# A shorter run-up on TensorE and a shorter way to the score bias, in a planned attention-plus-MLP kernel

## The chip, the cores and the metric

The kernel runs on one core of one Trainium2 chip. The metric is the device time of one execution in microseconds (us). TensorE (PE) multiplies; its weight loads are listed apart as PEld. VectorE is DVE, ScalarE is ACT, GpSimd is POOL, and SyncE (SP) issues nearly all DMAs.

## The reference

Windowed attention over 8 batches of 8 heads, 576 tokens of 64 numbers, is followed by a two-layer MLP with a squared ReLU over all 4608 tokens. Condensed:

```python
scores = scale * np.matmul(q, k.transpose(0, 1, 3, 2))
mask = np.abs(pos[:, None] - pos[None, :]) <= 32
scores = np.where(mask, scores, -1000000000.0)
attn = softmax(scores)                       # rows
x = (attn @ v) as [4608, 512]
h = x @ w_in                                 # 512 -> 2048
g = s * np.maximum(h, 0) ** 2 + b
out = g @ w_out                              # 2048 -> 512
```

## The kernel before

Nothing in this kernel is a loop on the chip. Python code calls `add(...)` once for each piece of work (a "task"), with the engine that does it, an estimated cost in ns, the tiles it reads and writes, and a key that breaks ties. `_Graph.plan` then plays the tasks through on a clock of estimates: it always takes the task that can start earliest, and of several the one with the lowest key. The order in which the plan takes them becomes the fixed program order of each engine, and `_Graph.emit` puts a semaphore wait where a task needs the result of another engine. So a changed cost or dependency moves tasks in the queues, and an engine that waits holds everything behind it in its own queue. Two rules of `emit` matter here: PE does not wait for PE, since it works in order; and each POOL task waits for the POOL task before it.

The start of the program is the part that the change touches.

- **Run-up.** DVE writes the all-ones tile ONESW (L463), and PE multiplies it with itself 26 times, 128 columns each (L486), into bank 1 of W. Nobody reads the result.
- **Constant tiles.** The helper `band` (L468 to L475) makes a 0/1 band by two POOL affine selects from ONESW. It makes the identity IDENT (for transposes) and MASK (the window of 32 on either side). From MASK, POOL computes NEG (L484), which is 0 inside the window and -1e38 outside. Copies of MASK with cuts (L501, L504) are for later units. Ahead of all this POOL fills two scratch tiles of `early` (L1028, L1029).
- **Batch 0, pairs of heads.** For each of four pairs, q and k are loaded (L579), cast to bf16 (`turn_pair`, L588 and L589: q on ACT once, then on POOL; k on DVE), transposed on PE against IDENT into W bank 0 for q and bank 1 for k (L595), and copied out as QT by ACT (L600) and KT by DVE (L601).
- **Scores of batch 0** (`pair_scores`). PE first writes NEG into the score bank: IDENT times NEG, two matmuls of 512 columns (L817), into SC for pairs 0 and 2 and into O for pairs 1 and 3; two more open AVN for the odd last tile (L822). The scores are then added on top (L826), so that the exponential (`first_exp`, L848) needs no mask. Batch 1 and later multiply the exponential by MASK on DVE (L853, L716).
- **Units of batch 0** (`first_units`). Five units of attention times V (L742), with a reciprocal and a scaling on DVE (L764, L766), a transpose on PE (L773) and a copy to XT on ACT (L781). V is loaded by L562 and cast by L571.
- **First MLP blocks.** Four short token blocks (96, 128, 128, 160 tokens) run the first layer (`s1`, L973, then L980 on ACT and L982 on DVE) while the weights still arrive: w_in and w_out in eight loads each (L534), cast on POOL (L537). `early` runs their second layer (L1022), and L1030, a sum over all of w_out for the constant term of the output, needs all eight w_out casts.
- **Batch 1 and later.** The pairs of batch 1 come through the same staging buffers (eight of them) as the weights, so an SP load waits until the cast of the earlier user is done. From batch 2 on, loads are paced by finished units, and PE alternates between L973 and L991, the second layer.

Of the kernel before, what the change touches and what calls it, by code (L numbers as in the profile page):

```python
# [9 lines left out]
ALU = mybir.AluOpType  # L10
# [6 lines left out]
WIN = 32  # L17
NPAIR = H // 2
NTILE = S // 64
# [31 lines left out]
TURN_DVE = ()  # L51
WARM = 26
LEAST = 2.0 ** -60
# [263 lines left out]
def bass_sliding_window_symmetric__then__act_starrelu_kernel(  # L317
# [23 lines left out]
    with ExitStack() as es:  # L341
# [125 lines left out]

        def band(tile, src, res, lo, hi, key, step=1):  # L468
            add("pool",
                lambda e: e.affine_select(tile, src, pattern=[[1, 128]],  # L470
                                          compare_op=ALU.is_ge, fill=0.0, base=-lo,
                                          channel_multiplier=-step),
                300, reads=["ONESW"], writes=[res], key=key)
            add("pool",
                lambda e: e.affine_select(tile, tile, pattern=[[-1, 128]],  # L475
                                          compare_op=ALU.is_ge, fill=0.0, base=hi,
                                          channel_multiplier=step),
                300, reads=[res], writes=[res], key=key)

        band(IDENT[:, :], ONESW[:, :], "IDENT", 0, 0, -98)  # L480
        for p0 in (0, 64):
            band(MASK[p0:p0 + 64, :], ONESW[p0:p0 + 64, :], ("MASK", 0, p0), 0, 64, -96)

        add("pool", lambda e: e.tensor_scalar(NEG[:, :], MASK[:, :], 1.0, FAR, ALU.subtract, ALU.mult), 250,  # L484
            reads=[("MASK", 0, 0), ("MASK", 0, 64)], writes=["NEG"], key=-95.5)
        add("pe", [lambda e: e.matmul(W[:, 1, 0:128], lhsT=ONESW[:, :], rhs=ONESW[:, :], start=True, stop=True)] * WARM,  # L486
            110.0 * WARM, reads=["ONESW"], writes=[("W", 1)], key=-99)

# [10 lines left out]

        for i, cuts in ((1, ((0, 96), (64, 0))), (2, ((64, 96),)), (3, ((0, 0),))):  # L500
            add("pool", lambda e, i=i: e.tensor_copy(MASKS[i][:, :], MASK[:, :]), 250,  # L501
                reads=[("MASK", 0, 0), ("MASK", 0, 64)], writes=[("MASK", i, 0), ("MASK", i, 64)], key=0.0)
            for p0, c0 in cuts:
                add("pool", lambda e, i=i, p0=p0, c0=c0: e.memset(MASKS[i][p0:p0 + 64, c0:c0 + WIN], 0.0), 150,  # L504
                    writes=[("MASK", i, p0)], key=0.0)
        for i in range(2):
# [77 lines left out]
        def turn_pair(b, name, pr, key, banks, eng, slack):  # L584
# [11 lines left out]
                view[p0:p0 + 64, i, :], nat[p0:p0 + 64, i * 64:i * 64 + 64], IDENT[p0:p0 + 64, p0:p0 + 64])  # L596
                for i in range(ROWS) for p0 in (0, 64)], 500.0, reads=[("NAT", ni), "IDENT"], writes=[res], key=key)
            flat = QT[slot][:, pr, WIN:WIN + S] if name == "q" else KT[slot][:, pr, :]
# [209 lines left out]
        def pair_scores(b, pr):  # L808
# [5 lines left out]
            if b == 0:  # L814
                wide = NEG.rearrange("p (one c) -> p one c", one=1)
                four = wide.to_broadcast((128, 4, 128))
                add("pe", [lambda e, hp=hp: e.matmul(bank[:, hp, :].rearrange("p (a c) -> p a c", a=4), lhsT=IDENT[:, :],  # L817
                                                     rhs=four, start=True, stop=True, skip_group_check=True)
                           for hp in (0, 1)], 440, reads=["NEG", "IDENT"], writes=[(name, 0), (name, 1)], key=-80.0 + pr)
                if pr == 0:  # L820
                    half = wide[0:64].to_broadcast((64, 4, 128))
                    add("pe", [lambda e, hp=hp: e.matmul(  # L822
                        AVN[0:64, hp, :].rearrange("p (a c) -> p a c", a=4), lhsT=IDENT[0:64, 0:64],
                        rhs=half, start=True, stop=True, skip_group_check=True) for hp in (0, 1)],
                        440, reads=["NEG", "IDENT"], writes=[("AVN", 0), ("AVN", 1)], key=-79.5)
            fns = [lambda e, j=j, hp=hp: e.matmul(  # L826
# [6 lines left out]
            key = (-30.0 if b == 0 else due(1, 0) - 3.5) + (1.0 if b == 0 else 0.1) * pr  # L833
            add("pe", fns, 450.0 if b == 0 else 500.0, reads=[("QT", b, x, pr) for x in range(NTILE)] +
                [("KT", b, x, pr) for x in range(NTILE)] + [("QTZ", b, 0), ("QTZ", b, WIN + S)],
# [49 lines left out]
        def attention():  # L885
# [15 lines left out]
            for t in ORDER0:  # L901
# [3 lines left out]
                else:  # L905
                    w("in", t - 8)
            first_units()
            for i, src in enumerate((moe_s, moe_b)):
                add("sp", lambda e, i=i, src=src: e.dma_start(SROW[0:128:32, i:i + 1], src.partition_broadcast(4)),
# [104 lines left out]
        def early():  # L1014
# [12 lines left out]
            even, block = OUTS[NOUT - 2][:, 0:128], OUTS[NOUT - 1][:, :]  # L1027
            add("pool", lambda e: e.memset(even, 1.0 / 32), 150, writes=[("OUTS", NOUT - 2)], key=-26.0)  # L1028
            add("pool", lambda e: e.memset(block, 0.0), 500, writes=[("OUTS", NOUT - 1)], key=-26.0)  # L1029
            add("pe", [lambda e, fc=fc, x=x: e.matmul(  # L1030
# [289 lines left out]
```

## Time and profile before

| what | value |
|---|---|
| runs | 317.33, 317.98, 321.23 us; median 317.98 us |
| profiled execution | 316.62 us, of which the span is 314.9 us |
| mean granted TensorE clock in it | 0.984 |
| busy share of the span | PE 96%, DVE 60%, ACT 45%, POOL 29% |
| share of PE in the chain that ended last | 86% |
| first DMA issue, first PE matmul | 0.80 us, 1.12 us |

The profile gives times from the start of the span. A row of the timeline is: start, duration in us, engine, line of the kernel, operation, what it writes and reads, how many such instructions are merged, and in brackets the idle time of the engine before it with what ended it. Matmuls are pipelined and their ends are modelled, so starts are firmer than ends. A row of the windows view gives the busy time of each engine in a stretch, then the clock that TensorE was granted in it (1.00 is full speed), the share of the DMA engines and GB/s.

### The profile page before, as it was taken

To read this page: it belongs to the slowest core of one execution; us is meant where nothing else is said; L and a number is where in the kernel's file an instruction comes from. 1 tells how busy PE (TensorE), PEld (TensorE's weight loads), DVE (VectorE), ACT (ScalarE), POOL (GpSimd) and SP (SyncE) were. 2 spreads that over 40 slices of the span, in tenths; PEclk is the share of its full clock that TensorE was granted. 3 is DMA by queue.
4 is the path that set the end of the run, shared out by engine and by line. 5 is a ranking of instruction groups with operands and counts; after the bars stand their busy time and mean duration, and the time that the engine had idled before them with its cause. 6 is when DMAs were issued, how large, how long until landed. Compare 5 with 4: busy or idle time off the path is not lost.

```text
span 314.9 us, 8371 instructions
## 1 busy us (share of the span) xinstructions
PE 303.8 (96%) x3559; PEld 158.6 (50%) x3559; DVE 189.6 (60%) x376; ACT 140.6 (45%) x219; POOL 90.5 (29%) x106
## 2 busy tenths in 40 slices
PE   7689999999999999999999999999999999999996
PEld 5478864544554544544444444444444444444444
DVE  2457686598886796686588666856455543333312
ACT  3636536257635765644354445444444333333300
POOL 7366853743334217142321601333000000000000
PEclk9959999999999999999999999999999999999999
DMA  7999999979998998999999799996211110010022
GB/s 252 296 278 392 386 311 301 187 151 312 233 152 242 242 165 199 287 162 139 269 225 186 180 220 291 143 181 129 72 54 52 52 46 34 33 37 33 34 88 83
DMA packets 98985, 56.13 MB, mean 178 GB/s; under 512 B 74048, under 2 KB 88128, under 8 KB 98944
## 3 DMA queue, kind: packets, MB, share of 16 engines
q1 hardware_dynamic: 98944, 55.56, 75.4%
q8 instruction: 29, 0.48, 0.7%
q14 instruction: 12, 0.10, 0.1%
HBM read 36.70 MB, written 9.44 MB: 147 GB/s over the span
## 4 chain that ended last, share of the span: by engine, by line
PE 86%; DMA 6%; DVE 3%; SPq 2%; issue 1%; ACT 1%
PE w L973 38%; PE o L991 33%; DMA stg<-in_k_dram 5%; PE avn L742 4%; PE o L1022 2%; PE avn L1022 2%; PE sc L684 2%; DMA vst<-in_v_dram 1%; SPq L625 1%; PE sc L742 1%; PE w L595 1%; PE avn L773 1%; SPq L579 1%; DVE xn L766 1%; PE sc L826 1%
## 5 line engine op out<-in xcount | busy, mean ns | idle before, releaser
L973 PE MATMUL w<-xt,win 128*128 128x512 bf16 (+3 forms) x768 | 145.5, 330 | 0.1
L980 ACT ACTIVATE r<-w 128x512 bf16<-128x512 f32 (+2 forms) x148 | 86.6, 586 | 104.9 <-PE w L973 90.9
L991 PE MATMUL o<-wout,gt 128*128 128x512 bf16 (+1 forms) x528 | 126.7, 373 | 0.0
L982 DVE TENSOR_TENSOR gt<-r 128x512 bf16<-128x512 bf16 (+2 forms) x148 | 77.4, 529 | 80.4 <-ACT r L980 79.7
L973 PEld LDWEIGHTS w<-xt,win 128*128 128x128 bf16 x768 | 63.5, 100 | 55.8 <-ACT r L980 0.8
L991 PEld LDWEIGHTS o<-wout,gt 128*128 128x128 bf16 x528 | 51.1, 98 | 57.3 <-DVE gt L982 0.2
L633 POOL CAST nat<-stg 128x1024 bf16<-128x1024 f32 (+1 forms) x21 | 25.3, 1204 | 64.6 <-DMA stg<-in_q_dram 47.8
L650 POOL COPY kt<-ktr 128x512 bf16<-128x512 bf16 (+1 forms) x30 | 31.8, 1060 | 38.2 <-DMA ktr<-nat 36.7
L712 ACT ACTIVATE ex<-sc 128x1024 bf16<-128x1024 f32 (+1 forms) x29 | 29.6, 1022 | 22.7 <-PE avn L742 21.6
L1007 DVE SCALAR_TENSOR_TENSOR outs<-o,sb,cvec 128x512 f32<-128x512 f32 (+1 forms) x35 | 25.4, 728 | 11.7 <-PE o L991 11.7
L716 DVE TENSOR_TENSOR ex<-ex,mask 128x1024 bf16<-128x1024 bf16 (+1 forms) x29 | 21.8, 752 | 1.1
L766 DVE TENSOR_TENSOR xn<-avn,rec 128x512 bf16<-128x512 f32 (+1 forms) x30 | 20.6, 688 | 0.9
L742 PE MATMUL avn<-vb,ex 64*64 64x65 bf16 x920 | 19.5, 199 | 0.7 <-DVE ex L716 0.5
L742 PEld LDWEIGHTS avn<-vb,ex 64*64 64x64 bf16 x920 | 12.7, 108 | 13.9 <-issue 6.1
L571 DVE CAST vb<-vst 128x512 bf16<-128x512 f32 (+1 forms) x30 | 12.9, 435 | 1.7 <-DMA vst<-in_v_dram 1.7
L633 DVE CAST nat<-stg 128x1024 bf16<-128x1024 f32 (+1 forms) x15 | 11.7, 786 | 1.2 <-DMA stg<-in_k_dram 1.2
L684 PE MATMUL sc<-qt,kt 64*64 64x128 bf16 x440 | 11.7, 216 | 0.7 <-ACT xt L781 0.7
L764 DVE RECIPROCAL rec<-avn 128x8 f32<-128x8 f32 (+1 forms) x30 | 6.0, 201 | 7.6 <-PE avn L742 7.3
L537 POOL CAST win<-stg 128x1024 bf16<-128x1024 f32 x8 | 8.4, 1049 | 6.4 <-DMA stg<-in_moe_w_in_dram 6.4
L537 POOL CAST wout<-stg 128x1024 bf16<-128x1024 f32 x8 | 8.8, 1100 | 2.0 <-DMA stg<-in_moe_w_out_dram 1.7
L781 ACT COPY xt<-avn 128x512 bf16<-128x512 bf16 (+2 forms) x13 | 6.6, 519 | 5.9 <-PE avn L773 5.9
L1022 PE MATMUL o<-wout,gt 128*128 128x512 bf16 x32 | 9.3, 381 | 0.0
(88 smaller groups left out, 143.0 us busy)
## 6 DMA issues: line engine op xcount, KB each, us to landing
out_dram<-outs SPq DMA_DIRECT2D x35, 256.0 KB, 2.9
vst<-in_v_dram SPq DMA_DIRECT2D x32, 256.0 KB, 6.6
stg<-in_q_dram SPq DMA_DIRECT2D x6, 1024.0 KB, 6.5
stg<-in_k_dram SPq DMA_DIRECT2D x6, 1024.0 KB, 10.8
stg<-in_moe_w_in_dram SPq DMA_DIRECT2D x8, 512.0 KB, 7.0
stg<-in_moe_w_out_dram SPq DMA_DIRECT2D x8, 512.0 KB, 9.7
stg<-in_q_dram SPq DMA_DIRECT2D x8, 288.0 KB, 5.5
stg<-in_k_dram SPq DMA_DIRECT2D x8, 288.0 KB, 5.4
```

The lines of the kernel that those rows point to most:

```text
L633: add(eng, lambda e, x=x: e.tensor_copy(nat[0:top, 1024 * x:1024 * x + 1024].rearrange("p (i h d) -> p h i d", h=H, i=2), stg[0:top, :].re ...
L650: add("pool", lambda e, c=c, w=w: e.tensor_copy(KT[slot][:, :, c:c + w].rearrange("p a (s i) -> p a s i", i=4), KTR[slot][:, :, :, c // 4: ...
L712: add("act", lambda e, dst=flat_dst, src=flat_src: e.activation(dst, src, AF.Exp, bias=0.0, scale=0.125), 190 + 0.833 * 512 * len(hs), rea ...
L716: add("dve", lambda e, flat=flat, mask=mask: e.tensor_tensor(flat, flat, mask, ALU.mult), 130 + 0.53 * 512 * len(hs), reads=[("E", ei, hp, ...
L742: return [lambda e: e.matmul(av[64 * x:64 * x + 64, h, 0:D + 1], lhsT=buf[64 * g:64 * g + 64, h % 2, h // 2, c:c + 64], rhs=VB[64 * g:64 * ...
L766: add("dve", lambda e: e.tensor_tensor(XN[xi][0:p1, :].rearrange("p (a c) -> p a c", a=H), av[0:p1, :, 0:D], REC[ri][0:p1, :].rearrange("p ...
L973: add("pe", [lambda e, g=g, kc=kc: e.matmul(wt[:, g, :], lhsT=WIN_BF[:, kc, (f0 + g) * 128:(f0 + g + 1) * 128], rhs=XT[:, kc, t0 % XR:t0 % ...
L980: add("act", lambda e: e.activation(rt, wt, AF.Relu, bias=0.0, scale=1.0), 190 + 0.833 * ng * nt, reads=[("W", wb)], writes=[("R1", rb)], ...
L982: add("dve", lambda e: e.tensor_tensor(GT[gs][:, f0:f0 + ng, g0:g0 + nt], rt, rt, ALU.mult), 130 + 0.53 * ng * nt, reads=[("R1", rb)], wri ...
L991: add("pe", [lambda e, fc=fc: e.matmul(O[:, ob, 0:cn], lhsT=GT[gs][:, fc, g0:g0 + 128], rhs=WOUT_BF[:, fc, c0:c0 + cn], start=(fc == 0), s ...
L1007: add("dve", lambda e: e.scalar_tensor_tensor(OUTS[us][:, 0:cn], bank, SB128[:, 0:1], CVEC[:, c0:c0 + cn], ALU.mult, ALU.add), 200 + 1.07 ...
L1022: add("pe", [lambda e, fc=fc, bank=bank, gs=gs, g0=g0: e.matmul(bank, lhsT=GT[gs][:, fc, g0:g0 + 128], rhs=WOUT_BF[:, fc, :], start=(fc == ...
```

## The change

The run-up becomes five matmuls of 512 columns. NEG is no longer computed from MASK: DVE clears it, and POOL writes -1e38 outside the window by two selects for each half, right behind the two of IDENT. MASK, its copies and the two scratch fills of `early` move to the function `masks` or get a dependency, so that they may only start after the last unit of batch 0 was multiplied (`land["av", 0, NUNIT - 1]`). The NEG matmuls of pair 1 and later into SC and O depend on the k transposes of the pair before, so that O is no longer opened ahead of the first transposes. Several estimated costs of the plan change too.

```diff
-WARM = 26
+WARM = 5
...
-        def band(tile, src, res, lo, hi, key, step=1):
+        def band(tile, src, res, lo, hi, key, fill=0.0, waits=(), source="ONESW"):
             add("pool",
                 lambda e: e.affine_select(tile, src, pattern=[[1, 128]],
-                                          compare_op=ALU.is_ge, fill=0.0, base=-lo,
-                                          channel_multiplier=-step),
-                300, reads=["ONESW"], writes=[res], key=key)
+                                          compare_op=ALU.is_ge, fill=fill, base=-lo,
+                                          channel_multiplier=-1),
+                350, reads=[source], writes=[res], key=key, waits=waits)
...
+        add("dve", lambda e: e.memset(NEG[:, :], 0.0), 150, writes=[("NEG", 0), ("NEG", 64)], key=-98.5)
         band(IDENT[:, :], ONESW[:, :], "IDENT", 0, 0, -98)
         for p0 in (0, 64):
-            band(MASK[p0:p0 + 64, :], ONESW[p0:p0 + 64, :], ("MASK", 0, p0), 0, 64, -96)
-
-        add("pool", lambda e: e.tensor_scalar(NEG[:, :], MASK[:, :], 1.0, FAR, ALU.subtract, ALU.mult), 250,
-            reads=[("MASK", 0, 0), ("MASK", 0, 64)], writes=["NEG"], key=-95.5)
-        add("pe", [lambda e: e.matmul(W[:, 1, 0:128], lhsT=ONESW[:, :], rhs=ONESW[:, :], start=True, stop=True)] * WARM,
-            110.0 * WARM, reads=["ONESW"], writes=[("W", 1)], key=-99)
+            band(NEG[p0:p0 + 64, :], NEG[p0:p0 + 64, :], ("NEG", p0), 0, 64, -97, -FAR, source=("NEG", p0))
+        ones = ONESW.rearrange("p (one c) -> p one c", one=1).to_broadcast((128, 4, 128))
+        add("pe", [lambda e: e.matmul(W[:, 1, :].rearrange("p (a c) -> p a c", a=4), lhsT=ONESW[:, :], rhs=ones,
+                                      start=True, stop=True)] * WARM,
+            430.0 * WARM, reads=["ONESW"], writes=[("W", 1)], key=-99)
...
+        def masks(after):
+
+            for p0 in (0, 64):
+                band(MASK[p0:p0 + 64, :], ONESW[p0:p0 + 64, :], ("MASK", 0, p0), 0, 64, -24.0, waits=[after])
+            for i, cuts in ((1, ((0, 96), (64, 0))), (2, ((64, 96),)), (3, ((0, 0),))):
...
-                for i in range(ROWS) for p0 in (0, 64)], 500.0, reads=[("NAT", ni), "IDENT"], writes=[res], key=key)
+                for i in range(ROWS) for p0 in (0, 64)], 400.0, reads=[("NAT", ni), "IDENT"], writes=[res], key=key)
+            land["turn", b, name, pr] = g.tasks[-1]
...
-                           for hp in (0, 1)], 440, reads=["NEG", "IDENT"], writes=[(name, 0), (name, 1)], key=-80.0 + pr)
+                           for hp in (0, 1)], 440, reads=[("NEG", 0), ("NEG", 64), "IDENT"], writes=[(name, 0), (name, 1)], key=-80.0 + pr,
+                    waits=[land["turn", 0, "k", pr - 1]] if pr else [])
...
-            add("pe", fns, 450.0 if b == 0 else 500.0, reads=[("QT", b, x, pr) for x in range(NTILE)] +
+            add("pe", fns, 320.0 if b == 0 else 500.0, reads=[("QT", b, x, pr) for x in range(NTILE)] +
...
             first_units()
+            masks(land["av", 0, NUNIT - 1])
...
-            add("pool", lambda e: e.memset(even, 1.0 / 32), 150, writes=[("OUTS", NOUT - 2)], key=-26.0)
-            add("pool", lambda e: e.memset(block, 0.0), 500, writes=[("OUTS", NOUT - 1)], key=-26.0)
+            made = [land["av", 0, NUNIT - 1]]
+            add("pool", lambda e: e.memset(even, 1.0 / 32), 150, writes=[("OUTS", NOUT - 2)], key=-19.0, waits=made)
+            add("pool", lambda e: e.memset(block, 0.0), 500, writes=[("OUTS", NOUT - 1)], key=-19.0, waits=made)
```

More of the change, by code (lines that the diff above doesn't have):

```diff
@@ L474, in band @@
             add("pool",
                 lambda e: e.affine_select(tile, tile, pattern=[[-1, 128]],
-                                          compare_op=ALU.is_ge, fill=0.0, base=hi,
-                                          channel_multiplier=step),
-                300, reads=[res], writes=[res], key=key)
+                                          compare_op=ALU.is_ge, fill=fill, base=hi,
+                                          channel_multiplier=1),
+                350, reads=[res], writes=[res], key=key)
@@ L498, in mask_of @@
             return 3 if ends[:1] == [0] else 0
[L500 to L505, printed above, removed]
+        def masks(after):
+            for p0 in (0, 64):
+                band(MASK[p0:p0 + 64, :], ONESW[p0:p0 + 64, :], ("MASK", 0, p0), 0, 64, -24.0, waits=[after])
+            for i, cuts in ((1, ((0, 96), (64, 0))), (2, ((64, 96),)), (3, ((0, 0),))):
+                add("pool", lambda e, i=i: e.tensor_copy(MASKS[i][:, :], MASK[:, :]), 250,
+                    reads=[("MASK", 0, 0), ("MASK", 0, 64)], writes=[("MASK", i, 0), ("MASK", i, 64)], key=0.0)
+                for p0, c0 in cuts:
+                    add("pool", lambda e, i=i, p0=p0, c0=c0: e.memset(MASKS[i][p0:p0 + 64, c0:c0 + WIN], 0.0), 150,
+                        writes=[("MASK", i, p0)], key=0.0)
         for i in range(2):
@@ L824, in pair_scores @@
                         rhs=half, start=True, stop=True, skip_group_check=True) for hp in (0, 1)],
-                        440, reads=["NEG", "IDENT"], writes=[("AVN", 0), ("AVN", 1)], key=-79.5)
+                        440, reads=[("NEG", 0), ("NEG", 64), "IDENT"], writes=[("AVN", 0), ("AVN", 1)], key=-79.5)
             fns = [lambda e, j=j, hp=hp: e.matmul(
```

## The prediction

> **What bounds the kernel now.** I read the page first: PE is 96% busy and has 86% of the chain that ended last, so a gain counts only where it lets PE begin its dense work earlier. The slices show where PE is not dense: the first four, and in the third one the granted clock is halved.
>
> ```profile
> PE   7689999999999999999999999999999999999996
> ...
> PEclk9959999999999999999999999999999999999999
> DMA  7999999979998998999999799996211110010022
> ...
> q8 instruction: 29, 0.48, 0.7%
> ```
>
> The reader is to see that the edit lies wholly in slices 1 to 5 (7.9 us each), and that the DMA engines are full there as well. Then I read the timeline of the first 28 us.
>
> ```profile
> 1.12 2.96 PE L486 MATMUL w<-onesw 128*128 128x128 bf16 x26 [1.12 <-DVE onesw L463]
> ...
> 3.91 0.64 POOL L484 TENSOR_SCALAR neg<-mask 128x128 bf16<-128x128 bf16 x1
> ...
> 4.61 0.60 PE L817 MATMUL sc<-neg,ident 128*128 128x512 bf16 x2 [0.53 <-POOL neg L484]
> ...
> 6.23 0.76 PE L595 MATMUL w<-ident,nat 64*64 64x64 bf16 x36
> ...
> 6.68 0.66 POOL L589 CAST nat<-stg 128x576 bf16<-128x576 f32 x1
> ...
> 10.17 0.46 DVE L589 CAST nat<-stg 128x576 bf16<-128x576 f32 x1 [0.47 <-DMA stg<-in_k_dram]
> ...
> 13.59 0.31 PE L826 MATMUL sc<-qt,kt 64*64 64x128 bf16 x8 [1.65 <-issue]
> ...
> 17.45 0.61 POOL L571 CAST vb<-vst 128x512 bf16<-128x512 f32 x1
> ...
> 18.70 0.95 PE L742 MATMUL avn<-vb,ex 64*64 64x65 bf16 x32
> ```
>
> The run-up ends at 4.08 and PE then waits 0.53 us for NEG: POOL is the end of that race. The first transposes start at 6.23 although their casts were done at 4.49 (ACT) and 4.98 (DVE). The second q cast waits on POOL behind the mask copies (its data landed at 5.87). At 13.59 PE has stood 1.65 us in the middle of 18 score matmuls, for nothing that the profile names. The windows view adds the clock: 1.00 until 14, 0.50 from 16 to 24.
>
> ```profile
> 14.00:16.00 2.00, 1.45 (x41) 0.75 (x42) 0.00 (x0) 2.00 (x4) 1.38 (x3) 0.72 1.20 286
> 16.00:18.00 2.00, 1.55 (x48) 1.01 (x45) 1.60 (x4) 0.93 (x3) 1.87 (x3) 0.50 1.06 180
> ```
>
> Last, the timeline further on, to see what the gain runs into. The last w_out cast and the matmuls that need all of them:
>
> ```profile
> 39.85 1.04 POOL L537 CAST wout<-stg 128x1024 bf16<-128x1024 f32 x1 [0.36 <-DMA stg<-in_moe_w_out_dram]
> 41.74 1.08 PE L1030 MATMUL sc<-wout,onesw 128*32 128x128 bf16 x64
> ```
>
> That cast waits for its load, and loads follow the full DMA queue and not PE. PE reaches L1030 0.85 us after the cast's end (40.89).
>
> **The change, part by part.** *Run-up.* The 26 matmuls start 107 ns apart, 1.2 columns per ns. Five of 512 at that rate are 5 x 0.427 = 2.13 us, so PE is free at 1.12 + 2.13 = 3.25 instead of 4.08. No run-up matmul of 512 columns is in the trace; the bounds are 0.27 us (half of the 0.54 between the starts of the NEG pairs at 4.61 and 5.14) and 0.43. I take 0.43, the row of the same stage.
>
> *NEG.* Affine selects start 0.355 us apart (1.75, 2.11, 2.46). Without the scratch fills in front, the first can start when ONESW is there (1.07), say 1.12; six take 2.13, so NEG is there at 3.25 and not 4.55. The new DVE clear costs 0.17 (ONESW's row) while DVE has nothing else until 4.52. The NEG matmuls can start at 3.3 instead of 4.61. SC and AVN are four matmuls: 1.08 us by the rows at 4.61 and 5.14, 1.71 at the run-up's rate. First transposes at 4.55 (their cast's end) to 5.1, against 6.23: 1.1 to 1.7 us earlier. O's two matmuls (0.54) are not gone, they follow the k transposes and delay only pair 1, whose q is not there yet. PE needs no semaphore for that, so the edit is one of order; behind it in PE's queue is the second q.
>
> *POOL without masks.* The second q cast starts at 5.9 instead of 6.68 and its transposes at 6.6 instead of 7.49. Scores of pair 0: KT at 5.8 + 0.75 = 6.55, matmuls after those transposes at 7.05 instead of 8.59, 1.5 us earlier.
>
> *Where this goes.* The k data land at 7.12, 8.55 and 10.15, whatever PE does. The last k cast is 10.17 to 10.63 in both kernels. The third KT copy comes before it on DVE (9.85 to 10.6 behind the cast of 8.55, then cast, transposes 0.4) or after it, so the fourth KT copy starts between 11.5 and 11.86; before: 11.86. At the last pair 1.5 us have become 0 to 0.3. But then PE stood until 13.59, and this I expect to move. Section 3 has 29 instruction packets in 0.48 MB for 7118 PE instructions, about 250 each; the first starts at 10.91 and is over at 12.10 in the packet records. So I read the stall as PE out of program, at its 449th recorded instruction. The change removes 21 matmuls and 21 weight loads ahead of it. The same instruction count is then reached 21 matmuls later: past the rest of pair 2 (10) and O's NEG (2), in the ninth score matmul of pair 3. The packet is asked for when PE passes a certain count, about 8.0 to 8.4 in either kernel, so I leave its arrival at 13.2 to 13.6. Pair 2's exponential (1.02) runs during that wait, instead of after it; pair 3's starts at 13.9 and not 14.92. Gain 1.0 us, bounds 0.4 (same arrival, pair 3 split later) and 1.8 (no stall: 13.1).
>
> *Next.* Unit 2 needs the V cast that ends at 17.45 + 0.61 = 18.06; it started at 18.70. Of 1.0 us 0.6 remain, up to 0.9 if the plan sets the first L973 ahead of it. Work until 25 at the halved clock is unchanged.
>
> *Deferred POOL work.* Four selects 1.42, three copies 1.29 (0.43 each), four memsets 0.59, two scratch fills 0.86 by their start distances: 4.2 us into the stretch 25 to 41, where POOL idles 3.6 us (1.34 before the cast at 26.33, 0.2 to 0.4 before each of the others). At nothing late, L1030 lets 0.85 us through; with 0.6 us of casts late, 0.25. I take 0.6 in the middle. The first product with w_out (32.16, cast done at 31.38) allows 0.78. After 47 PE is dense and the gain is carried, since the later loads wait for finished units.
>
> **Sum.** 316.62 - 0.6 = 316.0 for a profiled execution. The median shown is 1.36 above that execution; 317.98 - 0.6 = 317.4.
>
> Two rules of the Trainium skill speak here, and the sum does without them. The rows are the 107 ns in the run-up and 16 matmuls of 128 columns in 1.89 us at 21.85 against 1.06 at 25.25. "TensorE: Matmul & The Clock Gate", section "What's actually happening", says that PE starts at half rate and needs some 3.4 us of sustained work to be let go, in windows that do not start with the kernel. That speaks against a run-up of 2.1 us; by it the early transposes could stay slow for one window, about 1.5 us as an estimate, which the k loads at 10.15 would hide: 317.4 to 318. "Runtime: NRT & Kernel Launch", section "Instruction fetch mechanics", holds that fetching is mostly hidden; the row with 1.65 us disagrees. By the rule pair 3 would gain 1.8, and the V cast would still cut that to 0.6.
>
> **Rivals.** *The clock holds.* Before the halving PE was busy 1.76 us of 3.42 (11.46 to 14.88); with the stall split it is busier. If full speed holds through 18.7 to 25.1, PE saves about half of 6.4 us, say 3.0. Past L1030 this gets only as far as other ready work is queued there: 25 of the 32 pairs of L1022 come after it, so the plan could. 2.6 us in all: 315.4. Against it: unit 2 still waits for V at 18.06, an idle stretch that keeps PE quiet.
>
> *Nothing arrives.* DMA decides at 10.15, 18.06 and 40.89, and late casts eat the 0.85: 318.0.
>
> *POOL waits for PE.* The first deferred select waits for unit 4's L742 (24.09 to 25.02 before); w_in and w_out casts queue behind it. The plan's clock knows neither the stall nor the halving, so it may set the select ahead of the cast that ran at 22.31. Then 14 casts x 1.04 + 4.2 from 25.1 on end at 43.9 instead of 40.89, and L1030 is 2.3 us late: 320.3. It decides from the point where the last cast is over 0.85 us late. For it: POOL is strictly in order. Against: PE has products to do meanwhile, and a select set one cast later costs nothing.
>
> **How the numbers follow.** Forecast 0.50, clock 0.17, nothing 0.15, POOL 0.18. The likeliest's own range is 316.6 to 318.2. For eight in ten I take 314.8 (the clock case with its uncertainty) to 320.2 (nearly all of the POOL case). Two per cent, about what a measurement of this kernel can tell from no change, is 6.4 us: faster than that would need more than all idle and slow time before 25 us, 0.04; slower, a POOL wait well beyond the price above or a plan that loses elsewhere, 0.06; within, 0.90.
>
> **What would show it.** Right: L486 x5 ends near 3.4, L817 starts near 3.3, first L595 near 5, L826 of pair 0 near 7, the issue wait inside the last L826 group, unit 2 of L742 at 18.1 or an L973 before it, L1030 near 41.1. Wrong: L817 still waiting for NEG after 4, no issue wait or one as long in pair 2, clock 1.00 from 16 to 24, or POOL idle before a select while weights lie landed.

## The result, and the profile after

The changed kernel is slower, by about one per cent.

| | before | after |
|---|---|---|
| median | 318.57 us (317.33 to 321.23, 20 runs) | 321.93 us (319.56 to 323.50, 20 runs) |
| ratio to before, 95% interval | 1 | 1.0101 [1.0077, 1.0124] |
| profiled execution, its span | 316.62, 314.9 us | 320.53, 318.7 us |

The ratios here and below leave out disturbed runs, so they can differ a little from the quotient of the medians. Most line numbers have moved: L973 is now L980, L1022 is L1029, L1030 is L1038, L742 is L747, L773 is L778, L817 is L822, L826 is L832 and L537 is L541. In the experiments they move again; go by the tiles.

The slices of the page, as before: PE's busy tenths, the granted clock, and DMA.

```profile
PE   8698899979999999999999999999999999999995
...
PEclk9959799979999999999999999999999999999999
DMA  7999999999995999899799799998112210010022
```

Before, there was one slice of low clock. Now there are three: the third (16 to 24 us), the fifth (32 to 40) and the ninth (64 to 72). The timeline of PE gives the start, row for row:

```profile
1.12 2.32 PE L485 MATMUL w<-onesw 128*128 128x512 bf16 x5 [1.12 <-DVE onesw L463]
3.58 1.03 PE L822 MATMUL sc<-neg,ident 128*128 128x512 bf16 x2
...
6.91 0.47 PE L599 MATMUL w<-ident,nat 64*64 64x64 bf16 x18
7.23 0.42 PE L832 MATMUL sc<-qt,kt 64*64 64x128 bf16 x16
...
12.64 0.31 PE L832 MATMUL o<-qt,kt 64*64 64x128 bf16 x8 [0.58 <-DVE kt L606]
13.47 0.31 PE L832 MATMUL o<-qt,kt 64*64 64x128 bf16 x8 [0.52 <-issue]
...
17.28 1.49 PE L980 MATMUL w<-xt,win 128*128 128x96 bf16 x16
18.69 0.94 PE L747 MATMUL avn<-vb,ex 64*64 64x65 bf16 x32
...
24.60 6.01 PE L980 MATMUL w<-xt,win 128*128 128x96 bf16 x96
33.12 0.49 PE L1029 MATMUL o<-wout,gt 128*128 128x512 bf16 x1 [2.51 <-POOL mask L508]
33.41 3.51 PE L980 MATMUL w<-xt,win 128*128 128x128 bf16 x32
```

The reader is to see a head start and its loss. The 96 matmuls of the first layer begin at 24.60; before, the same group began at 26.34. Then PE stands 2.51 us ahead of its first product with w_out, and the next 32 matmuls take 3.51 us, where before they took 1.95. The sum is -1.74 + 2.51 + 1.56 = +2.33, and L1038 indeed starts 2.38 us later, at 44.12 where L1030 started at 41.74. The timeline of POOL shows what stood in front of that product:

```profile
23.52 0.65 POOL L470 TENSOR_SCALAR_AFFINE_SELECT mask<-onesw 64x128 bf16<-64x128 bf16 x2 [0.51 <-PE o L747]
24.23 1.04 POOL L541 CAST win<-stg 128x1024 bf16<-128x1024 f32 x1
...
28.34 0.20 POOL L1036 MEMSET outs<- 128x128 f32 x1
...
29.75 0.53 POOL L1037 MEMSET outs<- 128x512 f32 x1
30.34 1.04 POOL L541 CAST win<-stg 128x1024 bf16<-128x1024 f32 x1
31.44 0.30 POOL L505 COPY mask<-mask 128x128 bf16<-128x128 bf16 x1
31.80 1.04 POOL L541 CAST wout<-stg 128x1024 bf16<-128x1024 f32 x1
```

The masks and fills sit between the casts. The first w_out cast starts at 31.80 (before: 30.34), although its data landed at 30.76 (before: 30.29). The profile names L508 as the releaser, but PE's weight loads for that product begin at 32.89, right behind the end of the cast at 32.84.

The second low-clock stretch, again from PE's timeline:

```profile
62.07 1.03 PE L1029 MATMUL avn<-wout,gt 128*128 128x512 bf16 x4
...
65.50 0.40 PE L778 MATMUL w<-ident,xn 128*128 128x128 bf16 x4 [0.79 <-DVE xn L771]
66.35 0.40 PE L778 MATMUL sc<-ident,xn 128*128 128x128 bf16 x4 [0.45 <-DVE xn L771]
67.42 0.64 PE L689 MATMUL sc<-qt,kt 64*64 64x128 bf16 x8 [0.68 <-ACT xt L786]
68.39 3.74 PE L980 MATMUL w<-xt,win 128*128 128x512 bf16 x11 [0.33 <-issue]
```

Before, two groups of four w_out products stood between the transposes and the waits were covered:

```profile
61.88 0.40 PE L773 MATMUL w<-ident,xn 128*128 128x128 bf16 x4
62.11 1.03 PE L1022 MATMUL o<-wout,gt 128*128 128x512 bf16 x4
62.98 1.03 PE L1022 MATMUL avn<-wout,gt 128*128 128x512 bf16 x4
63.84 0.39 PE L773 MATMUL sc<-ident,xn 128*128 128x128 bf16 x4
64.90 0.41 PE L684 MATMUL sc<-qt,kt 64*64 64x128 bf16 x8 [0.68 <-ACT xt L781]
65.25 2.76 PE L973 MATMUL w<-xt,win 128*128 128x512 bf16 x12
```

In the changed kernel those products are spent by 63. Nothing in the edit touches that place, but from its 56th task on PE has another order. The changed estimates alone make it: when the plan of the kernel before is worked through with three of them (400 for the transposes, 320 for the scores of batch 0, 2150 for the run-up), it gives PE the changed kernel's order there, task for task. This is arithmetic on the plan and not a run.

### The profile page after: what moved, and what is told of

Same layout as the page of the kernel before. It is cut to its first block, busy times and chain, and to the rows that moved or that the text cites. A ratio compares the mean times of both kernels' runs of the same rounds, so it can differ in the third digit from the quotient of the medians.

```text
span 318.7 us, 8292 instructions
## 1 busy us (share of the span) xinstructions
PE 299.8 (94%) x3494; PEld 158.9 (50%) x3538; DVE 187.1 (59%) x377; ACT 140.9 (44%) x219; POOL 90.7 (28%) x109
## 4 chain that ended last, share of the span: by engine, by line
PE 85%; DMA 5%; issue 2%; POOL 2%; DVE 2%; ACT 0%; SPq 0%; POOLq 0%
PE w L980 37%; PE o L998 35%; PE avn L747 4%; DMA stg<-in_moe_w_in_dram 3%; PE sc L689 2%; DMA vst<-in_v_dram 2%; PE o L1029 2%; PE avn L1029 2%; DVE outs L1014 1%; POOL win L541 1%; PE w L599 1%; PE avn L778 1%; DVE xn L771 1%; PE sc L832 0%; SPq L538 0%
## 5 line engine op out<-in xcount | busy, mean ns | idle before, releaser
L980 PE MATMUL w<-xt,win 128*128 128x512 bf16 (+3 forms) x741 | 142.6, 333 | 4.3 <-issue 2.9
L998 PE MATMUL o<-wout,gt 128*128 128x512 bf16 (+1 forms) x519 | 125.1, 372 | 1.0 <-issue 0.6
L989 DVE TENSOR_TENSOR gt<-r 128x512 bf16<-128x512 bf16 (+2 forms) x148 | 75.1, 513 | 82.5 <-ACT r L987 81.7
L980 PEld LDWEIGHTS w<-xt,win 128*128 128x128 bf16 x768 | 65.7, 102 | 57.0 <-issue 2.2
L747 PE MATMUL avn<-vb,ex 64*64 64x65 bf16 x920 | 19.5, 199 | 0.2
L747 PEld LDWEIGHTS avn<-vb,ex 64*64 64x64 bf16 x920 | 12.7, 108 | 13.3 <-issue 6.4
L1029 PE MATMUL o<-wout,gt 128*128 128x512 bf16 x29 | 8.3, 383 | 2.7 <-POOL mask L508 2.5
L541 POOL CAST win<-stg 128x1024 bf16<-128x1024 f32 x8 | 8.4, 1044 | 2.2 <-DMA stg<-in_moe_w_in_dram 1.7
L1029 PE MATMUL avn<-wout,gt 128*128 128x512 bf16 x27 | 8.1, 380 | 0.7 <-issue 0.6
L541 POOL CAST wout<-stg 128x1024 bf16<-128x1024 f32 x8 | 8.3, 1042 | 0.7
```

The costliest lines, as they stand in the source:

```text
L747: return [lambda e: e.matmul(av[64 * x:64 * x + 64, h, 0:D + 1], lhsT=buf[64 * g:64 * g + 64, h % 2, h // 2, c:c + 64], rhs=VB[64 * g:64 * ...
L980: add("pe", [lambda e, g=g, kc=kc: e.matmul(wt[:, g, :], lhsT=WIN_BF[:, kc, (f0 + g) * 128:(f0 + g + 1) * 128], rhs=XT[:, kc, t0 % XR:t0 % ...
L989: add("dve", lambda e: e.tensor_tensor(GT[gs][:, f0:f0 + ng, g0:g0 + nt], rt, rt, ALU.mult), 130 + 0.53 * ng * nt, reads=[("R1", rb)], wri ...
L998: add("pe", [lambda e, fc=fc: e.matmul(O[:, ob, 0:cn], lhsT=GT[gs][:, fc, g0:g0 + 128], rhs=WOUT_BF[:, fc, c0:c0 + cn], start=(fc == 0), s ...
L1029: add("pe", [lambda e, fc=fc, bank=bank, gs=gs, g0=g0: e.matmul(bank, lhsT=GT[gs][:, fc, g0:g0 + 128], rhs=WOUT_BF[:, fc, :], start=(fc == ...
```

## Experiments

Three theories were open. **A**: the deferred POOL work delays the casts. **B**: the new order on PE loses on its own. **C**: the short run-up costs clock. And the head start itself had to be followed. Marks, in us from the start of the span: the first weight load of the 96-matmul group, of the first w_out product, of the sum over w_out (L1030, L1038), of the second batch's scores, of the first MLP block of 512 columns, and the last weight load of all. One profile stands behind each row, and marks move without a change of code: up to the 96 group the code of e9, and of f0 further down, is that of the kernel before on every engine, yet the group comes at 27.24 and 27.19 and not at 26.30, behind a first half-clock stretch that ends at 26.50 and 25.69 and not at 25.12. So a single mark is good to about 1 us.

| kernel | 96 group | first w_out product | sum | scores | 512 block | last | half clock after 30 us |
|---|---|---|---|---|---|---|---|
| before | 26.30 | 32.12 | 41.74 | 46.78 | 65.24 | 311.52 | none |
| after | 24.56 | 32.89 | 44.12 | 49.30 | 67.98 | 315.00 | 33.26 to 36.67, 67.40 to 70.81 |
| e1 | 25.22 | 31.10 | 40.72 | 46.05 | 64.51 | 312.91 | 64.75 to 68.16 |
| e2 | 24.77 | 31.43 | 41.02 | 46.62 | 65.77 | 314.81 | 66.06 to 69.47 |
| e6 | 26.07 | 33.38 | 43.12 | 48.67 | 67.49 | 317.31 | 65.84 to 72.67 |
| e7 | 24.75 | 32.90 | 42.63 | 47.76 | 66.97 | 313.39 | none |
| e8 | 24.51 | 31.53 | 41.13 | 46.77 | 65.11 | 311.74 | none |
| e9 | 27.24 | 33.07 | 42.69 | 48.19 | 68.27 | 315.47 | 67.46 to 70.87 |

### e1: masks on POOL, but right behind NEG

```diff
             band(NEG[p0:p0 + 64, :], NEG[p0:p0 + 64, :], ("NEG", p0), 0, 64, -97, -FAR, source=("NEG", p0))
+        negdone = g.tasks[-1]
...
-            masks(land["av", 0, NUNIT - 1])
+            masks(negdone)
```

> The changed kernel, with the masks moved back: POOL makes MASK and its copies right behind NEG and waits for no unit (the two scratch fills stay deferred). TensorE's order is the same but for one swap of a first-layer group with a unit. Theory A (deferred POOL work is the loss): the first w_out cast starts near 31.0 us and not 31.80, TensorE's wait at the first second-layer product falls from 2.5 us to 1.4 or less, the clock is not halved at 33 to 36, and the median falls from 321.9 us to 317 to 319. Theory B (the loss is the new order of TensorE, which arrives early and spends its spare products early): the idle time at 64 to 68 us and the second halved stretch stay, and the median stays at 320.5 us or more. Price of the edit itself: the second q cast up to 1 us late.

Measured: 320.25 us (318.13 to 325.0), ratio 1.0071 [1.0040, 1.0102]. The first w_out product is at 31.10 and its wait is gone; the sum over w_out is 3.4 us earlier than in the changed kernel, and even 1.0 earlier than before. Yet most of the loss in time remains, and the half clock near 65 is still there. So A is real in the profile, but the 0.3% by which e1 lies under the changed kernel is within the two intervals.

### e2: masks and fills on DVE, order unchanged

MASK is read off NEG on DVE, early; the copies, cuts and scratch fills follow there. The queues of PE, ACT and SP are those of the changed kernel.

```diff
-        def masks(after):
-            ...
+        add("dve", lambda e: e.tensor_scalar(MASK[:, :], NEG[:, :], -1.0, None, ALU.is_ge), 200,
+            reads=[("NEG", 0), ("NEG", 64)], writes=[("MASK", 0, 0), ("MASK", 0, 64)], key=-57.5)
...
-            add("pool", lambda e: e.memset(block, 0.0), 500, ..., waits=made)
+            add("dve", lambda e: e.memset(block, 0.0), 500, writes=[("OUTS", NOUT - 1)], key=-57.1)
```

> The changed kernel, with MASK (from NEG by a comparison), its copies and the two scratch fills on VectorE, where it is idle before 4.4 us. TensorE's order is the same, row for row, so only POOL's queue differs. Theory A: the stretch 23 to 42 us on POOL holds nothing but casts, the first w_out cast starts within 0.1 us of its landing (about 30.5), TensorE waits 1.0 us or less there, no halved clock after 30 us, median 316.5 to 318. Theory B: TensorE still runs out at 64 to 68 us and the clock halves there, median 320 to 321.5.

Measured: 320.32 us (319.07 to 324.52), ratio 1.0064 [1.0030, 1.0097]. PE's timeline at the first w_out product:

```profile
31.66 0.38 PE L1026 MATMUL o<-wout,gt 128*128 128x512 bf16 x1 [0.76 <-POOL wout L539]
31.88 1.95 PE L977 MATMUL w<-xt,win 128*128 128x128 bf16 x32
```

The 2.51 us have become 0.76, now waited for a cast that itself follows its load, and the 32 matmuls are back at 1.95. The gain in time over the changed kernel is some 0.4%, which the two intervals just fail to tell from nothing, and less than the 3.1 us by which the sum over w_out came earlier: something behind it loses again. The time is the one that theory B forecast; A had 316.5 to 318.

### e3: the short run-up alone

```diff
-WARM = 26
+WARM = 5
...
-        add("pe", [lambda e: e.matmul(W[:, 1, 0:128], lhsT=ONESW[:, :], rhs=ONESW[:, :], start=True, stop=True)] * WARM,
-            110.0 * WARM, reads=["ONESW"], writes=[("W", 1)], key=-99)
+        ones = ONESW.rearrange("p (one c) -> p one c", one=1).to_broadcast((128, 4, 128))
+        add("pe", [lambda e: e.matmul(W[:, 1, :].rearrange("p (a c) -> p a c", a=4), lhsT=ONESW[:, :], rhs=ones,
+                                      start=True, stop=True)] * WARM,
+            430.0 * WARM, reads=["ONESW"], writes=[("W", 1)], key=-99)
```

> The kernel before, with the five 512-column run-up matmuls alone, cost in the plan included. NEG is still made from MASK and ready near 4.55 us, so the first NEG matmul stays near 4.6 and TensorE idles from 3.4. POOL's queue is that of before; TensorE's order changes. Theory A: within 1 us of before, 318 to 319.5. Theory B (an order planned earlier costs by itself): 320 or more. A short run-up that costs clock would show as a later end of the first halved stretch than 25.1 us.

Measured: 320.08 us (316.50 to 322.27), ratio 1.0039 [0.9998, 1.0080], profiled 317.3. Inconclusive: the interval touches 1 and holds the times of both theories. In its profile the half clock lasts two windows (17.32 to 24.14) instead of three, and the second batch's scores start at 46.78, as before.

### e6: the changed kernel with the long run-up

```diff
-WARM = 5
+WARM = 26
...
+        add("pe", [lambda e: e.matmul(W[:, 1, 0:128], lhsT=ONESW[:, :], rhs=ONESW[:, :], start=True, stop=True)] * WARM,
+            430.0 * 5, reads=["ONESW"], writes=[("W", 1)], key=-99)
```

> The changed kernel with the run-up of 26 matmuls of 128 columns again, planned at the same cost, so that every engine's order is that of the changed kernel. TensorE is free at 4.1 us and not 3.4, so the first transposes come about 0.6 us later. Theories A and B: within 1 us of the changed kernel, 321 to 322.5, with the wait of 2.5 us at the first second-layer product and both halved stretches. A third theory, that the shorter run-up itself costs clock later, says 318 to 319.

Measured: 322.51 us (320.57 to 323.57), ratio 1.0128 [1.0080, 1.0176]. Putting the long run-up back does not give the time back, so C falls as the cause of the loss. Two of the signs did not come: the wait at the first w_out product is 1.32 us, with no half clock at 33, and the half clock near 66 lasts two windows. The time lost is as large all the same.

### e7, e8, e9: PE's order exchanged

A list of task numbers, built into the kernel, makes the plan take PE's tasks in a given order from the 56th on. The first 55 are the same tasks in both kernels. The plan then fits DVE, ACT and SP to PE, so their order changes too; POOL's does not.

```diff
+        self.pe_order = None
...
+                    if s == "pe" and self.pe_order and t is not pes[self.pe_order[pe_at]]:
+                        continue
...
+        g.pe_order = PE_ORDER
```

e7 is the changed kernel with the order of before, and POOL's queue as in the changed kernel.

> The changed kernel, with TensorE's program order from its 56th task on (the first transposes of batch 1, about 45 us) taken from the kernel before; POOL's queue is row for row that of the changed kernel, so the masks stay deferred. So far, of 1.0 per cent lost, taking the masks off POOL gave back 0.4 and left the idle time and the halved clock at 64 to 69 us. Theory A (POOL): the wait of 2.5 us and its halved clock at 33 us stay; median 320.5 to 322. Theory B (order): no halved clock at 64 to 68 us, the wait at the first second-layer product stays, median 318.5 to 320. Both together: 319 to 320.

e8 is e2 (masks on DVE) with the order of before.

> The changed kernel with the masks and scratch fills on VectorE and the order of TensorE from its 56th task on as in the kernel before. Theory A and B each leave the other's part: if both act, both are gone here, the idle time at 62 to 66 us falls to 1 us, no halved clock after 30 us, and the median is 316.3 to 317.8, below the kernel before (318.3). If the order does not matter (A alone), it stays at 320.

e9 is the kernel before (run-up, NEG and POOL untouched) with the order of the changed kernel.

> The kernel before, with the order of TensorE from its 56th task on as in the changed kernel; its run-up, its NEG and its POOL queue are untouched. Theory B: the second-layer products of the short blocks are spent sooner, TensorE idles 2.5 us or more at 62 to 68 us, the clock is halved there once, and the median rises from 318.3 to 320 to 321.5. Theory A: 318 to 319.

Measured:

| kernel | PE order | masks | median us | ratio to before |
|---|---|---|---|---|
| after | new | POOL, deferred | 321.93 | 1.0101 [1.0077, 1.0124] |
| e7 | old | POOL, deferred | 319.51 | 1.0040 [1.0001, 1.0079] |
| e2 | new | DVE | 320.32 | 1.0064 [1.0030, 1.0097] |
| e8 | old | DVE | 319.10 | 1.0025 [0.9985, 1.0066] |
| e9 | new | as before | 320.46 | 1.0060 [1.0022, 1.0099] |

The order alone (PE's, with what the plan moves on DVE, ACT and SP to fit it) costs 0.6% in e9, where nothing else is changed, and 0.6% is what the old order gives back in e7. Both are clear of the noise. With masks on DVE it is 0.4%, which is not. e8 missed its forecast of 316.3 to 317.8. The windows view of e9 and then of e7 shows the place:

```profile
64.00:72.00 8.00, 5.10 (x47) 2.48 (x44) 4.76 (x9) 3.31 (x5) 4.08 (x6) 0.79 0.81 155
```

```profile
32.00:40.00 8.00, 6.82 (x97) 5.92 (x100) 4.11 (x7) 3.16 (x6) 7.32 (x12) 1.00 1.05 385
64.00:72.00 8.00, 7.10 (x64) 3.27 (x62) 7.02 (x13) 4.52 (x7) 2.44 (x5) 1.00 0.87 137
```

e9 has PE busy for 5.10 of 8 us and a mean clock of 0.79, e7 7.10 at full clock (before: 7.21). The waits behind this in e9 are at the places of those in the changed kernel: 0.79 and 1.03 us for `xn` on DVE (there 0.79 and 0.45) and 0.68 for `xt` on ACT, which was there before too. Then comes one window at half clock. For the deferred POOL work 0.4% is left, between the changed kernel and e2, and 0.15% between e7 and e8; neither is clear of the noise, since the intervals are some 0.2 to 0.4% wide on each side. So that B costs time is shown twice. That A costs time is shown in the profiles, by the wait and the half clock that go with it, and in the times only as what B leaves over; which of the two is the larger is not shown.

### Where the head start goes: f0 to f4

e8 has the head start (24.51 against 26.30) and neither loss, and still it is no faster than before. Its marks say where the head goes: of 1.79 us 0.59 are left at the first w_out product, 0.61 at the sum, none at the scores. PE's timeline of e8:

```profile
31.76 0.38 PE L1052 MATMUL o<-wout,gt 128*128 128x512 bf16 x1 [0.63 <-POOL wout L565]
...
44.11 1.12 PE L1067 MATMUL sc<-outs 128*128 128x512 f32 x2 [0.68 <-DVE outs L1064]
45.17 0.75 PE L623 MATMUL w<-ident,nat 64*64 64x64 bf16 x36
45.85 0.60 PE L1052 MATMUL o<-wout,gt 128*128 128x512 bf16 x2
46.77 0.42 PE L856 MATMUL sc<-qt,kt 64*64 64x128 bf16 x16 [0.32 <-DVE cvec L1069]
```

and POOL's casts of e8, each waiting for its load:

```profile
35.77 1.10 POOL L565 CAST wout<-stg 128x1024 bf16<-128x1024 f32 x1 [0.31 <-DMA stg<-in_moe_w_out_dram]
37.13 1.04 POOL L565 CAST wout<-stg 128x1024 bf16<-128x1024 f32 x1 [0.26 <-DMA stg<-in_moe_w_out_dram]
38.51 1.04 POOL L565 CAST wout<-stg 128x1024 bf16<-128x1024 f32 x1 [0.34 <-DMA stg<-in_moe_w_out_dram]
39.86 1.04 POOL L565 CAST wout<-stg 128x1024 bf16<-128x1024 f32 x1 [0.31 <-DMA stg<-in_moe_w_out_dram]
```

Before, these four started at 35.77, 37.11, 38.44 and 39.85. This pair can be compared closely, since the loads land at the same times in both: w_out's first at 30.29 and 30.34 (e8), its last at 39.79 and 39.81, the next batch's q and k at 40.56 and 41.30 against 40.56 and 41.28. The DMA engines' share is 1.02 to 1.06 in every 8 us from 24 to 48 in both. So the first part of the head is lost to the loads: PE cannot pass a cast that waits for them.

The last 0.61 us are lost on DVE. Before, and then in e8, the same three squarings `gt`:

```profile
39.19 0.57 DVE L982 TENSOR_TENSOR gt<-r 128x512 bf16<-128x512 bf16 x1 [0.64 <-ACT r L980]
40.51 1.35 DVE L982 TENSOR_TENSOR gt<-r 128x512 bf16<-128x512 bf16 x2 [0.75 <-ACT r L980]
```

```profile
38.57 3.31 DVE L1012 TENSOR_TENSOR gt<-r 128x512 bf16<-128x512 bf16 x3 [0.19 <-ACT r L1010]
```

They start 0.62 us earlier in e8 and end at the same time, 41.88 against 41.86. The two of 512 columns take 1.25 and 1.28 us in e8, each beside a w_out cast on POOL (38.51 to 39.55 and 39.86 to 40.90); before, they overlap those casts less and take 0.57 and 0.65. The copies of `outs`, for which PE waits 0.68 us in e8, then start at 42.88 in both. That the cast slows the squaring is read from these rows and was not tested by itself.

To test whether the loads take the head, the w_out loads were halved. In f0 to f4 the 43 transposing transfers of the later batches are plain ones from a tile of ones, so the later batches' results are other values; they are to be compared with each other, and up to 47 us with all kernels. f0 is the kernel before so changed.

```diff
-                    dst.rearrange("p i a s -> p (i a) s"), nat[p0:p0 + np_, :], transpose=True),
+                    dst.rearrange("p i a s -> p (i a) s"), ones_like(16, np_)),
```

> The kernel before, with the 43 transposing transfers of the later batches (first at about 59 us) replaced by plain transfers of a tile of ones into the same places, so the later batches' results are not the reference's. It is the base of the next three runs, whose time can be compared with it alone. Up to 47 us nothing is changed: the (0,1) block at 26.3 +- 0.3, bias products at 44.1 +- 0.3, second batch's scores at 46.8 +- 0.3. Both theories expect the same here.

f1 is e8 with the same transfers.

> The kernel of e8 (early -1e38 tile, masks on VectorE, TensorE's order as in the kernel before from its 56th task), with the same plain transfers as in f0. Both theories expect what e8 showed: the (0,1) block at 24.3 to 24.8, the bias products and the second batch's scores within 0.4 us of f0, and the time within 0.3% of f0.

f2 and f3 are f0 and f1 with half of each w_out load.

```diff
+            part = 2 if which == "in" else 1
-            add("sp", lambda e: e.dma_start(stg, src), 600.0, ...
+            add("sp", lambda e: e.dma_start(stg[:, 0:part, :], src[:, 0:part, :]), 600.0, ...
```

> f0 with each of the eight w_out loads bringing only the first half of its bytes (128x512 instead of 128x1024; the other half of the staging buffer holds an old w_in piece, so half of w_out is wrong). Order and costs on all engines are as in f0. Theory A (in the kernel before, TensorE and the loads reach 44 us together): TensorE is dense from the (0,1) block at 26.3 to the bias products, so they stay at 44.1 +- 0.3 and the second batch's scores at 46.4 to 46.8; the time stays within 0.3% of f0. Rival B (the loads alone set 44 us and TensorE has room): both marks move forward by 0.5 us or more and the time falls by 0.2% or more.

> f1 with the same halved w_out loads as f2. In e8 the head of 1.8 us at the (0,1) block had become 0 at the bias products, 44.11 against 44.12 us. Theory A (the loads, which keep the DMA engines full from 10 to 47 us and land at the same times in both kernels, absorb the head): with lighter loads the head lives on, the bias products start at 42.3 to 43.2 against 44.1 in f2, the second batch's scores at 45.0 to 45.8, and the time is 0.3 to 0.6% under that of f2. Rival B (the head is lost on the engines themselves, in VectorE's chain of copies and gating, whatever the loads do): bias products and scores within 0.4 us of f2 and the same time within 0.2%.

f4 is f0 with 52 run-up matmuls, planned at the old cost.

> f0 (plain transfers in the place of the 43 transposing ones of the later batches, whose results are thus not the reference's) with 52 run-up matmuls of 128 columns instead of 26, planned at the same cost, so that every engine's order stays: TensorE is free for the -1e38 tiles at about 6.7 us instead of 4.6. The sign to read is the way from the (0,1) block to the second batch's scores: 20.2 to 20.5 us in f0, f2 and the kernel before, 21.8 and 22.3 us in the two kernels with the head start and full loads. Theory A (TensorE and the loads reach 44 us together in the kernel before): a delay has no room; the (0,1) block comes 0.5 to 2 us later than in f0 (27.2), the way stays 20.0 to 20.6 us, and the time is 0.2 to 0.6% over f0's ratio to the kernel before (0.9997). Rival B (the loads alone set 44 us): the way shrinks by what the block is late, to 18.5 to 19.7 us, and the ratio stays within 0.2% of f0's.

Measured ("way" is from the 96 group to the second batch's scores; f4 was compared in another set of runs):

| kernel | 96 group | sum | scores | way | 512 block | median us | ratio to before |
|---|---|---|---|---|---|---|---|
| f0 | 27.19 | 42.63 | 47.37 | 20.18 | 66.96 | 318.29 | 0.9997 [0.9960, 1.0034] |
| f1 | 25.15 | 41.71 | 46.94 | 21.79 | 66.45 | 318.24 | 0.9988 [0.9961, 1.0015] |
| f2 | 26.67 | 42.12 | 47.10 | 20.43 | 65.41 | 317.51 | 0.9963 [0.9929, 0.9998] |
| f3 | 25.11 | 41.34 | 45.99 | 20.88 | 64.29 | 318.19 | 0.9969 [0.9930, 1.0008] |
| f4 | 27.46 | 42.91 | 48.06 | 20.60 | 66.37 | 318.39 | 1.0012 [0.9982, 1.0042] |

With full loads a head of 2.04 us (f1 against f0) is 0.43 at the scores. With lighter loads a head of 1.56 (f3 against f2) is 1.11 there, and 1.12 at the 512 block. PE's timeline of f3, where the two waits of e8 are gone (0.68 for `outs`, 0.32 for `cvec`):

```profile
43.71 1.13 PE L1071 MATMUL sc<-outs 128*128 128x512 f32 x2
44.77 0.76 PE L627 MATMUL w<-ident,nat 64*64 64x64 bf16 x36
45.45 0.60 PE L1056 MATMUL o<-wout,gt 128*128 128x512 bf16 x2
45.99 0.42 PE L860 MATMUL sc<-qt,kt 64*64 64x128 bf16 x16
```

So in the profiles the head depends on the loads, in two ways. In e2, e8 and f1 the sum starts 1.3 to 1.4 us behind the landing of the last w_out load, 1.04 of it the cast (before: 1.95), so no more of the head could be left there. And behind the sum the two long squarings `gt` take 1.24 and 1.25 us in f1, beside the casts, and 0.53 and 0.43 in f3. The rival of f3's forecast had the right engine for this second part, DVE, but not the "whatever the loads do". The bias products of f3 start at 43.71, later than the 42.3 to 43.2 expected, and half of that head was lost before the sum. And the times do not confirm it: f3 and f2 differ by 0.06% in ratio, where 0.3 to 0.6% was expected. Whether the 1.1 us that f3 still leads by at 64 us reach the end is open; an interval of 0.4% on each side cannot show 0.35%. A pair with full loads warns against taking the loads for the whole answer: e2 and e9 have the same order of PE from the 56th task on, e2 leads by 2.47 us at the 96 group, 1.57 at the scores and 2.50 at the 512 block, and their ratios are 1.0064 and 1.0060.

f0 and f1 missed their marks too: f0 was to be within 0.3 us of 26.3 and 46.8 and came at 27.19 and 47.37, and f1's 96 group was to come at 24.3 to 24.8 and came at 25.15.

f4 decides little. Its -1e38 products start 1.60 us later (6.20 against 4.60), but a stall of 1.65 us that the profile books as issue ends at 14.13 there, and only 0.27 us of delay are left at the 96 group. The way is 20.60, no shorter than in f0, so there was no room for what was left; but so small a delay is no test. f2 is 0.3% under f0, at the edge of its forecast and within the noise of the two; its PE is 0.5 us ahead at 26.67 already, before any w_out product, so this says nothing of the loads.

No version that computes the reference is shown to be faster than the kernel before; e8 comes level with it.

## Why the prediction was wrong

The forecast was 317.4 us, 0.6 under the median, with a range of 314.8 to 320.2. The time came out at 321.93, one per cent over the kernel before. Point by point:

- **Run-up and NEG: right.** PE was to be free at 3.25 and the first NEG matmul at 3.3; it started at 3.58. Two sizes were off: the selects on the cleared NEG start 0.43 us apart, not 0.355, so NEG was there at 3.53; and the SC pair took 1.03 us instead of 0.60. The first transposes came at 4.56, inside the 4.55 to 5.1.
- **Scores, and the stall: right.** Second q transposes at 6.91 (6.6), pair 0's scores at 7.23 (7.05). The stall moved from pair 2 to the ninth score matmul of pair 3, as predicted, with 0.52 us that the profile books as issue, and ends at 13.47 (13.2 to 13.6). By order of start it lies ahead of the 445th recorded instruction in the kernel before; the prediction counted 449. Pair 3's exponential started at 13.86 (13.9).
- **Gain at 26 us: undersized.** 0.6 to 0.9 were to be left; it was 1.74 between the two profiles, and more against the 27.2 that the same code showed in e9 and f0. A first-layer group came ahead of unit 2 at 17.28, as the prediction allowed, and the half clock ended at 23.02 instead of 25.12, two windows of 3.41 us and not three. Unit 2 itself stayed at 18.69.
- **Deferred POOL work: mis-sized.** The casts were to be 0.6 us late. The first w_out cast started 1.46 us late, 0.47 of it because the load landed later and 0.99 because POOL was still busy with an earlier cast, a scratch fill and a mask copy. That is beyond the 0.78 us of the first w_out product. What the prediction did not see is that an early PE makes the same lateness a longer idle stretch: PE was done at 30.6 and waited 2.51 us, and behind that the clock was halved for a window, which cost 1.56 us. In e1 and e2, where the first w_out cast starts at 29.72 and 30.20, that halving is gone.
- **"After 47 PE is dense and the gain is carried": this step failed.** It took the order of PE in the changed kernel as that of before. The new costs make another order, and it loses by itself: 1.0060 in e9, and 0.6% of the 1.0% between e7 and the changed kernel. Where PE was to be dense it ran out of w_out products by 63, waited for DVE and ACT, and had the clock halved from 67.40 to 70.81. I had priced every edit of tasks, and the edits of costs at nothing: "a plan that loses elsewhere" stands only in the 0.06 for slower than two per cent, without a price.
- **With the old order the gain would not have arrived either.** The sum set the gain against PE's density. But e8, with the head and without the losses, has its last w_out load at 39.81 against 39.79 and its second batch's scores at 46.77 against 46.78, and its ratio is 1.0025 [0.9985, 1.0066].

Of the rivals, *POOL waits for PE* had the right place, L1030 more than 2 us late (2.4 against 2.3 predicted), by another way than it said: not a select waiting for unit 4 ahead of a cast, but casts in the queue behind masks, an idle PE, and the clock. That the number fits is luck: the sum counts 14 casts from the one at 22.31 on, and there are 13 (five of w_in, eight of w_out), so its own terms give about 1.1 us late. Its time, 320.3, also lacked the order's share. *The clock holds* was wrong in sign: the first half-clock stretch did shorten, but two new ones came.

On the clock, the rows are these: in the changed kernel the windows before the halvings at 16.20, 33.26 and 67.40 had PE busy for 1.95, 0.90 and 1.44 of 3.41 us. The Trainium skill, "TensorE: Matmul & The Clock Gate", section "What's actually happening", has windows of 3413 ns, with which the stretches of 3.41, 6.83 and 10.24 us agree, and a re-throttle after an idle window. The rows differ on the latter: no window here was idle from end to end, and 1.95 busy of 3.41 did not prevent it.

## What to carry to other kernels

In a planned kernel an estimated cost is part of the change: compare the order of each engine's queue before and after, and run the new order on the old code, before crediting or blaming the work itself. A head start is worth only what the next shared limit leaves of it, so look at when the loads land, and not only at when the engine is dense. Small work that is moved out of the start onto an in-order engine with casts to do can cost more there than it saved, first by its own time and then by the clock that the idle TensorE loses.

## What was not expected of the hardware

- **A partly idle window can halve the clock.** Cut into windows of 3.41 us that are counted from a halving, the profiles show half clock behind windows in which PE was busy for 0.90 (after), 1.11 (e9), 1.44 (after), 1.76 (before), 1.95 (after), 2.16 (e2, from 11.45) and 2.17 us (e6, from 62.42). It stayed whole behind 2.09 (e6, from 31.71), 2.59 and 2.79 (e8). Busy time alone does not decide: behind 1.82 us with an idle stretch of 1.70 (e7) and 1.84 us (e2, from 89.95), both with tiles of 128x128, the clock stayed too. The 1.76, 1.95 and 2.16 were mostly tiles of 64x64. How the activity is weighed is not settled here.
- **PE stalls at a fixed count of instructions.** Counted over matmuls and weight loads, PE's stall lies ahead of the 444th or 445th recorded instruction in before, after, e6, e7, e8 and f0 to f4, though the run-ups of these kernels have 10, 52 or 104 such instructions; it lasts 0.51 to 1.65 us and ends between 13.36 and 14.13 us. In f4 this puts it among the transposes of the last pair. e1, e9 and e3 reach that count only at 13.7 us or later and do not stall there, and e2 pauses 0.31 us, until 13.36. So the place follows the count and not the work, and a PE that comes late enough does not stall: this is shown. That PE waits there for instructions is argued from it and from the packet records, since nothing was run that changes their fetching.
